# One-block expert visits with tokens as the stationary operand, and small and large visits in turn

## The chip, the cores and the metric

The kernel runs on one core of a Trainium2 chip. The metric is the device time of one launch in microseconds (us); the time before is the median of three runs.

## What is computed

Three stages follow one another: a retention attention (4 batches, 8 heads, 768 positions, head size 64), a dense layer with softplus (3072 tokens, 512 to 2048 to 512), and a mixture of experts with a skip gate. The change is in the last one. Cut to what matters:

```python
def _moe2_ref(x, w_skip, w_gate, w1, w2):
    do_compute = x @ w_skip > 0              # the other tokens pass through
    xc = x[do_compute]
    logits = xc @ w_gate
    e_idx = np.argmax(logits, axis=1)        # one of 8 experts
    gate_w = softmax(logits)[e_idx]
    for e in range(E):
        mask = e_idx == e
        h = np.maximum(xc[mask] @ w1[e], 0.0)        # 512 -> 1024
        y[mask] = gate_w[mask, None] * (h @ w2[e])   # 1024 -> 512
    out[do_compute] = xc + y
```

## The kernel before

The first two stages run in steps over 8 units of 384 tokens and end with every token's expert and place in a list of records. The last stage then makes nine **visits**. A visit is one expert with up to 4 blocks of 128 tokens; `CAPS = (4, 3, 2, 2, 1, 1, 1, 1)` sets the blocks of visits 1 to 8, ranked by the experts' loads, after a first visit of 4 blocks (`first`, visit 0) whose expert is known early. A loop for tokens beyond the caps stands at the end; the trace shows no pass of it.

One visit consists of:

- `load_w1`, `load_w2` (L142): 4 MB of weights, eight pieces of 512 KB, from SP's queue into a ring of ten raw slots. A load waits until the piece ten places before it has been split.
- `gather` (L163): one indirect DMA a block, issued by POOL, fetches token rows.
- `transposes` (L174) and `take` (L936, L937): TensorE turns the tokens of block j into PSUM bank `hp2[j]`; ScalarE copies them out as the high part `xh`, VectorE subtracts to get the low part `xl`.
- `split` (L154, L157): each raw piece becomes a high part `h` (ScalarE) and a low part `l = raw - h` (VectorE for w1, POOL for w2, the eng argument). `h` and `l` have rings of five slots for each layer.
- `ffn1` (L952): each product is the sum of three terms, x-high times w-high, x-high times w-low, x-low times w-high. The weights are the stationary operand (128x128) and the tokens of the visit the moving one, 128 to 512 columns: 96 matmuls whatever the number of blocks. ScalarE (L958) and VectorE (L959) bring the result out as `gh` and `gl`.
- `ffn2` (L968): for each block 24 matmuls with `gh`, `gl` stationary and 512 columns of w2 moving, into bank `op2[j]`.
- `ffn_out` (L976, L979): VectorE scales and adds, POOL scatters the rows to the output.

The order is written out by hand: within a visit, `ffn1` of this visit with the w1 splits of the next, then the next visit's `transposes`, `take` and w2 splits, then `ffn2`. Each engine takes its instructions in that order, so the position in the source sets what waits behind what. The visits run 0, 1, 2, ... 8: the four of one block come last.

```python
for i in range(4):
    ffn1(s, [i])
    if nxt:
        split_w1(nxt, i)
```

Of the kernel before, what the change touches and what calls it, by code (L numbers as in the profile page):

```python
# [38 lines left out]
RAWS, RINGS = 10, {"1": 5, "2": 5}  # L39

# [34 lines left out]
def retention_moe_moe2(ctx: ExitStack, tc: tile.TileContext, a: dict, out: bass.AP):  # L75
# [62 lines left out]

    def load(s, kind, i, src):
        t = s["r" + kind, i] = piece("raw", RAWS, F32)  # L140
        k = KD if kind == "1" else 2
        return nc.sync.dma_start(out=t.rearrange("p (k f) -> p k f", k=k), in_=src)  # L142

    def load_w1(s, e):
        return [load(s, "1", i, wsrc(w1, e)[:, :, i * 256:(i + 1) * 256]) for i in range(4)]
# [4 lines left out]
    def split(s, kind, i, eng, heng=None):  # L150
        r = s["r" + kind, i]
        h, lo = piece("h" + kind, RINGS[kind], F32R), piece("l" + kind, RINGS[kind], F32R)
        if heng is None:
            nc.scalar.activation(out=h, in_=r, func=AF.Copy)  # L154
        else:
            heng.tensor_copy(h, r)
        eng.tensor_tensor(out=lo, in0=r, in1=h.bitcast(F32), op=ALU.subtract)  # L157
        k = KD if kind == "1" else 2
        s["h" + kind, i], s["l" + kind, i] = (x.rearrange("p (k f) -> p k f", k=k) for x in (h, lo))
# [113 lines left out]
    with tc.manual_schedule():  # L273
# [634 lines left out]
        with ExitStack() as left:  # L908
# [9 lines left out]
            xgb.append(xg_p.tile([128, 4, DM], F32, name="xg2"))  # L918
            for n, s in enumerate(vis):
                s["xg"] = xgb[n % 3]  # L920
# [42 lines left out]
            def ffn2(s, blocks=None):  # L963
                for j in range(s["nb"]) if blocks is None else blocks:
                    js = slice(j * 128, (j + 1) * 128)
                    for f in range(NF2):
                        for n, (x, w) in enumerate((("gh", "h2"), ("gl", "h2"), ("gh", "l2"))):
                            nc.tensor.matmul(  # L968
                                op2[j], lhsT=s[x][:, f, js], rhs=s[w, f // 2][:, f % 2, :],
                                start=(f == 0 and n == 0), stop=(f == NF2 - 1 and n == 2),  # L970
                            )

            def ffn_out(s, blocks=None):
                for j in range(s["nb"]) if blocks is None else blocks:
                    op, o = op2[j], s["xg"][:, j, :]
# [65 lines left out]
            ev, _ = known(1)  # L1041
            load_w1(vis[1], ev)
# [14 lines left out]
            load_w2(vis[1], ev)  # L1057
            nc.gpsimd.memset(xgb[2], 0.0)
            gather(vis[1])
            gather(vis[2])  # L1060
            ffn2(first, (0, 1))
            ffn_out(first, (0, 1))
            transposes(vis[1])
            take(vis[1])
            for i in range(4):
                split_w1(vis[1], i)
            ffn2(first, (2, 3))
            ffn_out(first, (2, 3))
            nc.sync.dma_start(out=ovc, in_=a["c_ov"])
            for i in range(4):  # L1070
                split_w2(vis[1], i)
            ev, _ = known(2)
            load_w1(vis[2], ev)
            load_w2(vis[2], ev)
            for n in range(1, NV):
                s = vis[n]
                nxt = vis[n + 1] if n + 1 < NV else None
                if n + 2 < NV:
                    gather(vis[n + 2])
                for i in range(4):  # L1080
                    ffn1(s, [i])
                    if nxt:
                        split_w1(nxt, i)
                if n + 2 < NV:
                    ev, _ = known(n + 2)
                    load_w1(vis[n + 2], ev)
                if nxt:
                    transposes(nxt)
                    take(nxt)
                    for i in range(4):  # L1090
                        split_w2(nxt, i)
                if nxt is None:
                    nov, oti = overflow_table()
                ffn2(s)
                if n + 2 < NV:
                    load_w2(vis[n + 2], ev)
                ffn_out(s)

# [42 lines left out]
```

## Time and profile before

| what | value |
|---|---|
| median of 3 runs | 1042.31 us (1040.92 to 1043.36) |
| the profiled execution's own time | 1038.72 us |
| its span, first to last instruction | 1036.9 us |
| granted TensorE clock, mean over the span | 0.976 |
| busy: TensorE / its weight loads | 94% / 79% |
| busy: VectorE, POOL, ScalarE | 56%, 55%, 46% |
| DMA over the span | 97 GB/s |

The page gives busy shares for the whole span; the change touches only the part after about 805 us, so shares and waits are read from that part. "Chain" is the list of work that ended last, each piece followed back to what released it. In a timeline row, the number in brackets is the idle time of that engine just before, and what ended it.

### The profile page before, as it was taken

The page shows a single profiled execution, that of the slowest core. Times are in us where ns is not written, and L with a number is a line of the kernel's source. Part 1 is how long each engine was busy: PE and PEld are TensorE (multiplying, and loading weights), DVE is VectorE, ACT ScalarE, POOL GpSimd, SP SyncE. Part 2 cuts the span into 40 slices and gives each one's busy share as a digit, 9 for nine tenths or more (in the row PEclk, how much of TensorE's full clock was granted, in tenths as well). Part 3 has the DMA queues.
Part 4 walks back from the last instruction along what each step waited for, and adds up shares of the span by engine and source line. Part 5 has one row for each costly group of instructions (what it writes and reads, how often), then busy time and mean ns, then how long its engine had stood idle before and what let it go on. Part 6 is the DMA issues. An engine that isn't in the chain of part 4 may idle for free.

```text
span 1036.9 us, 16748 instructions
## 1 busy us (share of the span) xinstructions
PE 977.5 (94%) x5922; PEld 822.3 (79%) x5922; DVE 580.8 (56%) x1328; ACT 481.2 (46%) x947; POOL 566.5 (55%) x460
## 2 busy tenths in 40 slices
PE   7877888999999999999999999997989999999994
PEld 6766677888888888888888888886967788999994
DVE  6899995546444654644565465456327452444652
ACT  3554444445354544544544454454544342354650
POOL 5577765546644653654565465455553554366671
PEclk9999899999999999999999999999998999999997
DMA  8744343212310411321041141010054762556830
GB/s 224 189 125 130 101 108 100 46 35 66 88 39 9 117 30 39 100 47 39 12 118 29 27 115 31 9 62 2 1 188 157 256 211 83 173 196 207 258 102 9
DMA packets 186839, 100.50 MB, mean 97 GB/s; under 512 B 140594, under 2 KB 167378, under 8 KB 186752
## 3 DMA queue, kind: packets, MB, share of 16 engines
q1 hardware_dynamic: 182176, 89.56, 31.8%
q0 software_dynamic: 4144, 9.04, 2.6%
q8 instruction: 48, 0.79, 0.3%
q10 hardware_dynamic: 432, 0.79, 0.2%
q14 instruction: 39, 0.32, 0.1%
HBM read 83.43 MB, written 17.85 MB: 98 GB/s over the span
## 4 chain that ended last, share of the span: by engine, by line
PE 67%; DVE 15%; issue 7%; ACT 4%; POOL 4%; DMA 2%; SPq 0%; POOLq 0%; DVEq 0%; ACTq 0%
PE ac L664 20%; PE hp L616 20%; PE hp L952 9%; PE op L968 8%; PE sc L438 3%; PE y L460 3%; DVE lo L652 2%; DVE m L320 2%; DVE m L316 2%; DVE m L324 2%; DVE t L636 1%; DVE g L645 1%; PE y L458 1%; PE tp L689 1%; POOL ln L638 1%
## 5 line engine op out<-in xcount | busy, mean ns | idle before, releaser
L638 POOL TENSOR_TENSOR ln<-ln,t 128x384 f32<-128x384 f32 x127 | 149.7, 1179 | 260.9 <-ACT ln L630 234.0
L664 PE MATMUL ac<-wo,hi 128*128 128x512 f32 x768 | 276.3, 414 | 9.3 <-ACT hi L646 9.3
L616 PE MATMUL hp<-xth,wi 128*128 128x384 f32 x1024 | 212.6, 349 | 0.2 <-ACT xth L484 0.2
L616 PEld LDWEIGHTS hp<-xth,wi 128*128 128x128 f32 x1024 | 176.4, 189 | 12.9 <-ACT xth L484 0.6
L664 PEld LDWEIGHTS ac<-wo,hi 128*128 128x128 f32 x768 | 147.5, 192 | 48.1 <-ACT hi L646 11.1
L628 ACT ACTIVATE u<-hp 128x384 f32<-128x384 f32 x128 | 62.7, 490 | 238.0 <-PE hp L616 219.3
L664 PE MATMUL ac<-wo,lo 128*128 128x512 f32 x384 | 154.7, 403 | 5.0 <-DVE lo L652 4.5
L639 POOL TENSOR_TENSOR ln<-ln,u 128x384 f32<-128x384 f32 x127 | 153.1, 1205 | 10.0
L652 DVE TENSOR_TENSOR lo<-g,hi 128x384 fp32r<-128x384 f32 x128 | 98.2, 767 | 67.4 <-ACT hi L646 65.0
L157 POOL TENSOR_TENSOR l<-raw,h 128x1024 fp32r<-128x1024 f32 x34 | 80.7, 2398 | 65.8 <-ACT h L154 65.7
L616 PE MATMUL hp<-xtl,wi 128*128 128x384 f32 x512 | 109.5, 334 | 0.0
L636 DVE TENSOR_SCALAR t<-u 128x384 f32<-128x384 f32 x128 | 54.0, 422 | 95.6 <-ACT u L629 92.1
L154 ACT ACTIVATE h<-raw 128x1024 fp32r<-128x1024 f32 x71 | 73.2, 1057 | 38.5 <-issue 33.2
L616 PEld LDWEIGHTS hp<-xtl,wi 128*128 128x128 f32 x512 | 90.6, 188 | 0.0
L664 PEld LDWEIGHTS ac<-wo,lo 128*128 128x128 f32 x384 | 74.0, 193 | 20.8 <-DVE lo L652 8.9
L646 ACT ACTIVATE hi<-g 128x384 fp32r<-128x384 f32 x128 | 67.3, 525 | 41.8 <-DVE g L645 35.4
L477 DVE TENSOR_TENSOR wsb<-wps,wsb 64x64 f32<-64x64 f32 x112 | 24.8, 221 | 93.7 <-PE wps L469 93.0
L645 DVE TENSOR_TENSOR g<-g,ln 128x384 f32<-128x384 f32 x128 | 71.6, 559 | 0.9 <-POOL ln L639 0.9
L630 ACT ACTIVATE ln<-u 128x384 f32<-128x384 f32 x128 | 67.4, 527 | 4.1
L629 ACT ACTIVATE u<-u 128x384 f32<-128x384 f32 x128 | 67.2, 525 | 4.1
L958 ACT ACTIVATE gh<-hp 128x128 fp32r<-128x128 f32 (+3 forms) x72 | 28.5, 397 | 77.5 <-PE hp L952 72.9
L157 DVE TENSOR_TENSOR l<-raw,h 128x1024 fp32r<-128x1024 f32 x38 | 55.5, 1470 | 12.3 <-ACT h L154 9.6
(199 smaller groups left out, 1637.1 us busy)
## 6 DMA issues: line engine op xcount, KB each, us to landing
raw<-in_moe_w SPq DMA_DIRECT2D x72, 512.0 KB
raw<-in_moe_w_in SPq DMA_DIRECT2D x16, 512.0 KB
raw<-in_moe_w_out SPq DMA_DIRECT2D x16, 512.0 KB
kn<-in_k SPq DMA_DIRECT2D x56, 96.0 KB
vn<-in_v SPq DMA_DIRECT2D x56, 96.0 KB
x1d<-x SPq DMA_DIRECT2D x21, 256.0 KB
out<-x SPq DMA_DIRECT2D x21, 256.0 KB
ks<-in_k SPq DMA_DIRECT2D x96, 48.0 KB
```

What stands on the lines that cost most here:

```text
L154: nc.scalar.activation(out=h, in_=r, func=AF.Copy)
L157: eng.tensor_tensor(out=lo, in0=r, in1=h.bitcast(F32), op=ALU.subtract)
L616: nc.tensor.matmul(hp, lhsT=wi[:, f, w, kk, :], rhs=x[:, kk, :], start=(n == 0), stop=(n == 3 * KD - 1),)
L630: nc.scalar.activation(out=ln, in_=u, func=AF.Ln, bias=1.0)
L638: eng.tensor_tensor(out=ln, in0=ln, in1=t, op=ALU.subtract)
L639: eng.tensor_tensor(out=ln, in0=ln, in1=u, op=ALU.add)
L645: nc.vector.tensor_tensor(out=g, in0=g, in1=ln, op=ALU.add)
L646: nc.scalar.activation(out=hi, in_=g, func=AF.Copy)
L652: nc.vector.tensor_tensor(out=lo, in0=g, in1=gh[T, f].bitcast(F32), op=ALU.subtract)
L664: nc.tensor.matmul(ac[T, j], lhsT=x[:, js], rhs=wo[:, f, w, :], start=(f == 0 and n == 0), stop=(f == NF - 1 and n == 2),)
L952: nc.tensor.matmul(hp2[(2 * i + g) % 4][:, 0:w], lhsT=wt[:, kk, g * 128:(g + 1) * 128], rhs=x[:, kk, 0:w], start=(n == 0 and kk == 0), sto ...
L968: nc.tensor.matmul(op2[j], lhsT=s[x][:, f, js], rhs=s[w, f // 2][:, f % 2, :], start=(f == 0 and n == 0), stop=(f == NF2 - 1 and n == 2),)
```

## The change

Visits are taken in pairs, a one-block visit and a larger one: (5, 1), (6, 2), (7, 3), (8, 4). In a one-block visit the first layer is `ffn1x`: 128 tokens are the stationary operand and 512 columns of w1 the moving one, so its w1 pieces are loaded by rows of the contraction (4 KB runs) instead of by columns. The result has tokens on partitions, so ScalarE writes `gs` (relu), and `turn` transposes eight 128x128 squares of it into `hp2[0]` and `hp2[1]`, from which `gh` and `gl` are made. The second layer of a one-block visit uses `op2[3]`. Between the two halves of the second layer of the previous large visit stand `turn` and the large visit's own transposes. Two of the four w1 splits of a small visit go to POOL, three of its four w2 splits, and two of the four w2 splits of a large visit (before: no w1 split, all four w2 splits of every visit after the first).

```diff
+PAIRS = ((5, 1), (6, 2), (7, 3), (8, 4))
...
+    def parts_of(s, kind):
+        return 2 if kind == "2" else 1 if s["nb"] == 1 else KD
+
     def load(s, kind, i, src):
         t = s["r" + kind, i] = piece("raw", RAWS, F32)
-        k = KD if kind == "1" else 2
-        return nc.sync.dma_start(out=t.rearrange("p (k f) -> p k f", k=k), in_=src)
+        return nc.sync.dma_start(out=t.rearrange("p (k f) -> p k f", k=parts_of(s, kind)), in_=src)
 
     def load_w1(s, e):
-        return [load(s, "1", i, wsrc(w1, e)[:, :, i * 256:(i + 1) * 256]) for i in range(4)]
+        w = wsrc(w1, e)
+        if s["nb"] == 1:
+            return [load(s, "1", i, w[:, i:i + 1, :]) for i in range(KD)]
+        return [load(s, "1", i, w[:, :, i * 256:(i + 1) * 256]) for i in range(4)]
...
-            xgb.append(xg_p.tile([128, 4, DM], F32, name="xg2"))
-            for n, s in enumerate(vis):
-                s["xg"] = xgb[n % 3]
+            xgs = [xg_p.tile([128, 1, DM], F32, name=f"xs{i}") for i in range(2)]
+            for n, (a1, b1) in enumerate(PAIRS):
+                vis[a1]["xg"], vis[b1]["xg"] = xgs[n % 2], xgb[(n + 1) % 2]
+            gs = g_p.tile([128, F2], F32, name="gs")
...
-            def ffn2(s, blocks=None):
+            def ffn1x(s, kk):
+                for g in range(2):
+                    for n, (x, w) in enumerate((("xh", "h1"), ("xh", "l1"), ("xl", "h1"))):
+                        nc.tensor.matmul(
+                            hp2[2 + g], lhsT=s[x][:, kk, 0:128], rhs=s[w, kk][:, 0, g * 512:(g + 1) * 512],
+                            start=(kk == 0 and n == 0), stop=(kk == KD - 1 and n == 2),
+                        )
+
+            def ffn1x_out():
+                for g in range(2):
+                    nc.scalar.activation(out=gs[:, g * 512:(g + 1) * 512], in_=hp2[2 + g], func=AF.Relu)
+
+            def turn(s):
+                s["gh"] = g_p.tile([128, NF2, 128], F32R, name="gh1")
+                s["gl"] = g_p.tile([128, NF2, 128], F32R, name="gl1")
+                for b in range(2):
+                    for f in range(4):
+                        nc.tensor.transpose(hp2[b][:, f * 128:(f + 1) * 128], gs[:, (4 * b + f) * 128:(4 * b + f + 1) * 128], ident)
+                for b in range(2):
+                    fs, tv = slice(4 * b, 4 * b + 4), hp2[b].rearrange("p (f t) -> p f t", f=4)
+                    nc.scalar.activation(out=s["gh"][:, fs, :], in_=tv, func=AF.Copy)
+                    nc.vector.tensor_tensor(out=s["gl"][:, fs, :], in0=tv, in1=s["gh"][:, fs, :].bitcast(F32), op=ALU.subtract)
+
+            def ffn2(s, blocks=None, ops=None):
                 for j in range(s["nb"]) if blocks is None else blocks:
                     js = slice(j * 128, (j + 1) * 128)
-                    for f in range(NF2):
+                    op = op2[3 if s["nb"] == 1 else j]
+                    for f in range(NF2) if ops is None else ops:
                         for n, (x, w) in enumerate((("gh", "h2"), ("gl", "h2"), ("gh", "l2"))):
                             nc.tensor.matmul(
-                                op2[j], lhsT=s[x][:, f, js], rhs=s[w, f // 2][:, f % 2, :],
+                                op, lhsT=s[x][:, f, js], rhs=s[w, f // 2][:, f % 2, :],
                                 start=(f == 0 and n == 0), stop=(f == NF2 - 1 and n == 2),
                             )
 
             def ffn_out(s, blocks=None):
                 for j in range(s["nb"]) if blocks is None else blocks:
-                    op, o = op2[j], s["xg"][:, j, :]
+                    op, o = op2[3 if s["nb"] == 1 else j], s["xg"][:, j, :]
...
+            def fetch(n, which):
+                if n not in ids:
+                    ids[n] = known(n)[0]
+                (load_w1 if which == 1 else load_w2)(vis[n], ids[n])
+
+            fetch(PAIRS[0][0], 1)
...
-            load_w2(vis[1], ev)
-            nc.gpsimd.memset(xgb[2], 0.0)
-            gather(vis[1])
-            gather(vis[2])
+            fetch(PAIRS[0][1], 1)
+            for x in xgs:
+                nc.gpsimd.memset(x, 0.0)
+            gather(vis[PAIRS[0][0]])
+            gather(vis[PAIRS[0][1]])
             ffn2(first, (0, 1))
             ffn_out(first, (0, 1))
-            transposes(vis[1])
-            take(vis[1])
+            s1, b1 = (vis[n] for n in PAIRS[0])
+            transposes(s1)
+            take(s1)
             for i in range(4):
-                split_w1(vis[1], i)
-            ffn2(first, (2, 3))
-            ffn_out(first, (2, 3))
-            nc.sync.dma_start(out=ovc, in_=a["c_ov"])
-            for i in range(4):
-                split_w2(vis[1], i)
-            ev, _ = known(2)
-            load_w1(vis[2], ev)
-            load_w2(vis[2], ev)
-            for n in range(1, NV):
-                s = vis[n]
-                nxt = vis[n + 1] if n + 1 < NV else None
-                if n + 2 < NV:
-                    gather(vis[n + 2])
+                split_w1(s1, i, nc.gpsimd if i % 2 else nc.vector)
+            ffn2(first, (2,))
+            ffn_out(first, (2,))
+            big = first
+            for m, (ns, nb) in enumerate(PAIRS):
+                s, b = vis[ns], vis[nb]
+                nxt = PAIRS[m + 1] if m + 1 < len(PAIRS) else None
+                fetch(ns, 2)
+                for kk in range(KD):
+                    ffn1x(s, kk)
+                    split_w1(b, kk)
+                ffn1x_out()
+                if m == 0:
+                    last = (3,)
+                    ffn2(big, last, range(4))
+                else:
+                    last = (big["nb"] - 1,)
+                    ffn2(big, range(big["nb"] - 1))
+                    ffn_out(big, range(big["nb"] - 1))
+                if nxt:
+                    gather(vis[nxt[0]])
+                turn(s)
+                split_w2(s, 0)
+                transposes(b)
+                take(b)
+                ffn2(big, last, range(4, NF2) if m == 0 else None)
+                for i in range(1, 4):
+                    split_w2(s, i, nc.gpsimd if i % 2 else nc.vector)
+                ffn_out(big, last)
+                if m == 0:
+                    nc.sync.dma_start(out=ovc, in_=a["c_ov"])
+                if nxt:
+                    fetch(nxt[0], 1)
+                fetch(nb, 2)
+                if nxt:
+                    fetch(nxt[1], 1)
                 for i in range(4):
-                    ffn1(s, [i])
+                    ffn1(b, [i])
                     if nxt:
-                        split_w1(nxt, i)
-                if n + 2 < NV:
-                    ev, _ = known(n + 2)
-                    load_w1(vis[n + 2], ev)
+                        split_w1(vis[nxt[0]], i, nc.gpsimd if i % 2 else nc.vector)
                 if nxt:
-                    transposes(nxt)
-                    take(nxt)
-                    for i in range(4):
-                        split_w2(nxt, i)
-                if nxt is None:
-                    nov, oti = overflow_table()
-                ffn2(s)
-                if n + 2 < NV:
-                    load_w2(vis[n + 2], ev)
+                    gather(vis[nxt[1]])
+                    transposes(vis[nxt[0]])
+                    take(vis[nxt[0]])
+                for f in range(0, NF2, 2):
+                    ffn2(s, ops=(f, f + 1))
+                    split_w2(b, f // 2, nc.gpsimd if f % 4 else nc.vector)
                 ffn_out(s)
+                big = b
+            nov, oti = overflow_table()
+            ffn2(big)
+            ffn_out(big)
```

How the order moves, at three places. First TensorE, in the first layer of a one-block visit (the last pieces of a visit; `hp` is a bank of results, `xh`, `xl` the tokens, `h`, `l` the w1 parts, the stationary operand stands last). Before, one output chunk after another:

```order
L952 MATMUL hp_0_8232<-xh_10472,h_0_10414 128x128 x4
L952 MATMUL hp_0_8232<-xh_10472,l_0_10415 128x128 x4
L952 MATMUL hp_0_8232<-xl_10473,h_0_10414 128x128 x4
L952 MATMUL hp_1_8233<-xh_10472,h_0_10414 128x128 x4
L952 MATMUL hp_1_8233<-xh_10472,l_0_10415 128x128 x4
L952 MATMUL hp_1_8233<-xl_10473,h_0_10414 128x128 x4
```

and now:

```order
L972 MATMUL hp_2_8234<-h_1_10125,xh_10139 128x512
L972 MATMUL hp_2_8234<-l_1_10126,xh_10139 128x512
L972 MATMUL hp_2_8234<-h_1_10125,xl_10140 128x512
L972 MATMUL hp_3_8235<-h_1_10125,xh_10139 128x512
L972 MATMUL hp_3_8235<-l_1_10126,xh_10139 128x512
L972 MATMUL hp_3_8235<-h_1_10125,xl_10140 128x512
```

A quarter of the layer was 24 matmuls of 128 columns and is 6 of 512. Second, TensorE in the fourth pair, between the two blocks of the previous visit's second layer (`gs` is the result to be turned, `xg` the gathered tokens of the large visit):

```order
L998 MATMUL op_0_8446<-h_2_10179,gl_10000 128x512
L998 MATMUL op_0_8446<-l_2_10180,gh_9999 128x512
L986 MATMUL hp_0_8232<-cst,gs 128x128 x4
L986 MATMUL hp_1_8233<-cst,gs 128x128 x4
L179 MATMUL hp_0_8232<-cst,xg_8259 128x128 x4
L179 MATMUL hp_1_8233<-cst,xg_8259 128x128 x4
L998 MATMUL op_1_8447<-h_4_10149,gh_9999 128x512
L998 MATMUL op_1_8447<-h_4_10149,gl_10000 128x512
```

The same two banks are filled twice in a row: the second filling has to wait until the first has been read. Third, VectorE from the end of pair three to that place:

```order
L163 TENSOR_TENSOR l_4_10150<-raw_9973,h_4_10149 128x1024
L163 TENSOR_TENSOR l_1_10170<-raw_9977,h_1_10169 128x1024
L1006 SCALAR_TENSOR_TENSOR xs_8377<-op_3_8570,rc_8787,xs_8377 128x512
L163 TENSOR_TENSOR l_2_10202<-raw_9991,h_2_10201 128x1024
L163 TENSOR_TENSOR l_3_10212<-raw_9993,h_3_10211 128x1024
L163 TENSOR_TENSOR l_4_10222<-raw_9995,h_4_10221 128x1024
L163 TENSOR_TENSOR l_0_10232<-raw_9997,h_0_10231 128x1024
L1006 SCALAR_TENSOR_TENSOR xg_8260<-op_0_8446,rc_8699,xg_8260 128x512
L990 TENSOR_TENSOR gl_10266<-hp_0_8232,gh_10265 128x512
L990 TENSOR_TENSOR gl_10266<-hp_1_8233,gh_10265 128x512
```

The two `gl` rows that free the banks now stand behind six splits on VectorE, while POOL has the splits between them.

## Rows read from the trace of the kernel before

**Rows 1.** The page, busy time of the whole span.
```profile
PE 977.5 (94%) x5922; PEld 822.3 (79%) x5922; DVE 580.8 (56%) x1328; ACT 481.2 (46%) x947; POOL 566.5 (55%) x460
```

**Rows 2.** Chain from 820 us: start, length (us), engine, tile, line, count.
```profile
909.99 11.51 PE hp L952 x96
...
956.18 10.67 PE hp L952 x96
966.85 0.46 PE hp L174 x4
967.31 5.48 PE op L968 x24
...
989.40 2.64 PE hp L952 x24
...
997.63 0.04 issue
...
1000.57 0.46 PE hp L174 x4
```

**Rows 3.** Timeline of `ffn2`, weight load and matmul: start, length (us), engine, line.
```profile
985.15 0.19 PEld L968 LDWEIGHTS op<-h,gl 128*128 128x128 f32 x1
985.15 0.39 PE L968 MATMUL op<-h,gh 128*128 128x512 f32 x1
```

**Rows 4.** Groups by form, 820 us to the end: busy us, mean ns of one.
```profile
L154 ACT ACTIVATE h<-raw 128x1024 fp32r<-128x1024 f32 x64 | 66.2, 1058 | 38.5 <-issue 33.2 <-PE op L968 4.3 <-ACT h L154 1.0
...
L976 DVE SCALAR_TENSOR_TENSOR xg<-op,rc,xg 128x512 f32<-128x512 f32 x15 | 11.3, 751 | 52.2 <-PE op L968 47.4 <-POOL l L157 4.8
...
L937 DVE TENSOR_TENSOR xl<-hp,xh 128x512 fp32r<-128x512 f32 x15 | 9.7, 683 | 0.0
...
L936 ACT ACTIVATE xh<-hp 128x512 fp32r<-128x512 f32 x14 | 7.7, 596 | 0.0
```

**Rows 5.** Timeline at the hand-over from visit 0 to visit 1.
```profile
816.72 1.47 PE L174 MATMUL hp<-cst,xg 128*128 128x128 f32 x12
...
819.20 2.07 ACT L936 ACTIVATE xh<-hp 128x512 fp32r<-128x512 f32 x4 [12.57 <-PE hp L174]
819.59 0.66 PE L174 MATMUL hp<-cst,xg 128*128 128x128 f32 x4 [1.41 <-DMA xg<-x1d,rc]
```

**Rows 6.** Line 157 on VectorE and on POOL: ns shortest/median/longest.
```profile
L157 DVE TENSOR_TENSOR l<-raw,h x38: 1209/1225/5555, 779.5 to 1001.9; 128x1024 fp32r<-128x1024 f32 x38
L157 POOL TENSOR_TENSOR l<-raw,h x34: 2367/2396/2479, 797.7 to 1010.4; 128x1024 fp32r<-128x1024 f32 x34
```

**Rows 7.** Timeline of visit 7: four POOL splits, and VectorE beside them.
```profile
986.91 9.42 POOL L157 TENSOR_TENSOR l<-raw,h 128x1024 fp32r<-128x1024 f32 x4
...
991.03 0.29 DVE L959 SCALAR_TENSOR_TENSOR gl<-hp,gh 128x128 fp32r<-128x128 f32 x1 [0.84 <-ACT gh L958]
...
993.32 4.10 DVE L157 TENSOR_TENSOR l<-raw,h 128x1024 fp32r<-128x1024 f32 x1 [0.66 <-ACT h L154]
...
997.67 0.52 PEld L952 LDWEIGHTS hp<-xh,h 128*128 128x128 f32 x4 [0.43 <-DVE gl L959]
```

**Rows 8.** Stretches: length, busy PE, PEld, DVE, ACT, POOL, clock, DMA share, GB/s.
```profile
945.00:956.00 11.00, 11.00 (x51) 9.11 (x50) 3.00 (x4) 5.81 (x7) 5.29 (x3) 1.00 0.52 159
...
973.00:984.00 11.00, 11.00 (x100) 10.96 (x100) 8.13 (x12) 5.29 (x12) 7.85 (x4) 1.00 0.82 239
984.00:990.00 6.00, 6.00 (x32) 5.08 (x30) 2.49 (x4) 4.99 (x6) 4.64 (x3) 1.00 0.88 295
```

**Rows 9.** Waits of SP's queue, 760 us to the end: us, times, longest.
```profile
SPq L142 <- POOL l L157: 80.6, 26, 15.4
```

**Rows 10.** Timeline, the last matmul and the last scatter.
```profile
1022.33 0.39 PE L968 MATMUL op<-l,gh 128*128 128x512 f32 x1
...
1023.79 0.99 POOL L979 DMA_INDIRECT out<-xg,rc  x1 [9.87 <-DVE xg L976]
```

**Rows 11.** Timeline of POOL, a gather that waits for an earlier scatter.
```profile
966.73 1.05 POOL L163 DMA_INDIRECT xg<-x1d,rc  x1 [3.22 <-DMA out<-xg,rc]
```

More of the change, by code (lines that the diff above doesn't have):

```diff
@@ L157, in split @@
         eng.tensor_tensor(out=lo, in0=r, in1=h.bitcast(F32), op=ALU.subtract)
-        k = KD if kind == "1" else 2
-        s["h" + kind, i], s["l" + kind, i] = (x.rearrange("p (k f) -> p k f", k=k) for x in (h, lo))
+        s["h" + kind, i], s["l" + kind, i] = (x.rearrange("p (k f) -> p k f", k=parts_of(s, kind)) for x in (h, lo))
     def gather(s, rows=NT):
@@ L1040, in retention_moe_moe2 @@
             split_w1(first, 3)
-            ev, _ = known(1)
-            load_w1(vis[1], ev)
+            ids = {}
+            def fetch(n, which):
[3 more added lines that the diff above has]
+            fetch(PAIRS[0][0], 1)
             ffn1(first, [1])
```

## The prediction

> **What bounds the kernel now.** I began with the page: TensorE is busy 94% of the span, no other engine over 56% beside its weight loads [rows 1]. That is an average over three stages, so I read the chain of the stage that changes. From 820 us it is TensorE, piece after piece without gaps: first layer, transposes, second layer, next visit [rows 2]. The reader should compare two of its lengths. The second layer of one block takes 5.48 us for 24 matmuls, 0.228 us each; the first layer of the same block takes 10.67 us for 96 matmuls, 0.111 us each. The multiplications are as many. Each matmul has its own weight load of 0.19 us, laid over the matmul before it [rows 3]: with 512 columns moving it is hidden, with 128 it leaves the array half idle. So TensorE sets the end here, and its first layer in the four one-block visits is twice as long as the arithmetic asks. The one long gap is the hand-over from visit 0 to visit 1: 1.41 us until a gather lands [rows 5]. DMA runs at 239 to 295 GB/s where SP has free slots [rows 8], and TensorE does not wait for it; SP waits for slots, 80.6 us of it on POOL's splits [rows 9].
>
> **The change, part by part.**
>
> *First layer of four one-block visits.* Before: three times 10.67 us, and once 11.17 us (989.40 to 1000.57, visit 7, with a stall) [rows 2], together 43.2 us. Now 24 matmuls each, with a weight load of 128x128 and 512 columns of fp32r, the form of the second layer; at its 5.48 us that is 21.9 us. Gain 21.3 us, all on the chain. (The Trainium skill, page "TensorE: Matmul & The Clock Gate", section "Back-to-back issue gap", gives a sustained spacing of about 81 ns at 128 columns and 131 ns at 512. By it the gain would be an estimated 4 x (96 x 81 - 24 x 131) ns = 18.5 us. The rows say 111 and 228 ns for this data type, and I go by them.)
>
> *Turning the result.* Eight transposes a visit; four take 0.46 us [rows 2], so 0.92 us, four times: 3.7 us lost.
>
> *The two banks filled twice.* `turn` fills `hp2[0]` and `hp2[1]`, and the large visit's transposes fill the same two at once after it. Before, `hp2[0]` had half a first layer's time to be emptied. Now the chain is: four transposes and their tail, about 0.63 us; ScalarE copies 0.60 us; VectorE subtracts 0.68 us [rows 4]; three hand-overs of 0.04 us [rows 2]: 2.03 us, while TensorE is ready after 0.92. Wait 1.1. The second bank is free 0.68 us later, at 2.72, and TensorE comes at 2.47: another 0.3. Together 1.4 us a pair, 5.6 us over four. Bounds: 0.9 us if the second wait hides, 2.5 us if one ScalarE split of 1.06 us [rows 4] gets ahead; I take 1.4, since nothing is queued on ScalarE between the relu and this copy. After it the second layer of the large visit's last block (5.48 us, 2.7 in pair 1) covers `take`.
>
> *Hand-over from visit 0.* Only one gather, not four, must land before the first transposes; it is issued first, and three gathers had landed by 816.72 us [rows 5]. The 1.41 us go.
>
> *The first small visit.* It starts 0.46 + 5.48 us after 816.72, at 822.7 us, one block's second layer earlier than visit 1's did. Its w1 pieces must be split by then. If ScalarE's copies start at 819.20 as in the row [rows 5], the four high parts end at 820.9 to 824.0, and the low parts, two on VectorE and two on POOL, which do not run together (see rivals), end with the third piece at up to 828.1; TensorE wants it at 825.6: 2.5 us. If the copies start when the transposes end, it is 0.7 us. I take 2.5, the end that a row shows.
>
> *Splits and slots.* Per pair 16 pieces on ScalarE at 1.06 us, nine on VectorE at 1.22, seven on POOL at 2.40 [rows 4, 6]: 17, 11 and 17 us under pairs of 36 us and more, so covered on the average. TensorE's pair 4, the shortest, is 5.48 (first layer) + 5.48 + 3.2 (turn, transposes, wait) + 5.48 + 11.51 (large first layer [rows 2]) + 5.48 = 36.6 us; pair 3, with one block more and the next visit's transposes, 42.5. I cost these moves at nothing. The cover is thinnest at pair 4's `turn`. Counted from the start of pair 3's small second layer: POOL ends its last w1 split at about 3.6 us, two gathers (1.3 us each with their issue [rows 11]) at 6.2 and two w2 splits at 11.0; if VectorE's four w1 splits wait for all of that, they end at 15.9. `turn` comes at 3 x 5.48 = 16.4, and VectorE's first subtraction there 1.3 us later.
>
> *Loads.* The order of loads is the order of splits, ten pieces ahead, as before; 8.4 MB a pair over 36.6 us is 229 GB/s, below the rates of [rows 8]. Nothing on the chain. The memsets before the first gathers shrink from one of 2048 to two of 512 columns, off the chain.
>
> *The end.* The last matmul, VectorE, the scatter 1.5 us after it [rows 10], and the rest of the span stay: the last block is now one of two, but its scatter is alone at the end.
>
> *Sum.* -21.3 + 3.7 + 5.6 - 1.4 + 2.5 = -10.9 us. The profiled execution goes from 1038.72 to 1027.8. It lies 3.6 us below the median of the runs shown, so for the median I say 1042.3 - 10.9 = **1031.4 us**.
>
> **The rivals.**
>
> *A. Splits that lock each other out.* VectorE's splits are usually 1.22 us, but one took 5.55 [rows 6]; one took 4.10 us, from 993.32 to 997.42, and came free when POOL's row of four ended at 996.33, after which TensorE waited 0.43 us [rows 7]. A subtraction from PSUM (0.29 us at 991.03) ran at full speed beside POOL. So a VectorE split waits for a whole run of POOL splits, and the change puts splits on both at once and the bank-freeing subtraction behind them. For it: a gather can hold POOL back 3.2 us first [rows 11]. Against it: in pairs 2 and 3 the margin is over 5 us. Price: POOL's run late by 3.2 us costs 3.2 - 1.8 = 1.4 us at pair 4's `turn`, and one POOL split of 2.4 us out of turn costs as much in the last second layer, which starts right behind the splits of its own weights; with one more stall of 0.4 us as in [rows 7], 4.2 us. Time 1035.6. (The Trainium skill, page "SBUF — State Buffer", section "Who interferes with whom", says that a VectorE instruction with two SBUF inputs and a GpSimd instruction that reads SBUF lock each other out for the whole instruction, whoever issues first. By that rule the trace agrees for VectorE. It also says that POOL waits in the other order; no row shows it, for POOL's 34 splits all take 2367 to 2479 ns.)
>
> *B. Slower: the transfers become the bound in pairs 3 and 4.* If loads came only at the 159 GB/s of the stretch 945 to 956 [rows 8], each pair would need 52.7 us, 10 and 16 us over TensorE's. Time 1042.3 - 10.9 + 26 = 1057. It decides below 187 GB/s (2 x 8.39 MB in 42.5 + 36.6 + 10.9 us). For it: slots are freed by later, mixed splits. Against: that stretch was short of slots, not of transfers, and 239 to 295 GB/s were reached just behind it.
>
> *C. The change does not do what it says:* a new weight for every matmul not hidden, 24 x (0.228 + 0.19) = 10 us, so that turning is lost outright: 1050. The second layer already changes its weight each time and shows 0.228 [rows 2, 3].
>
> *D. More gain:* start covered (0.7 us) and the second bank wait hidden (2 us): about 1028.
>
> *E. No change:* A and part of B together eat 11 us: 1042.
>
> **How the numbers follow.** My forecast 0.62, A 0.20, D 0.07, B 0.05, E 0.04, C 0.02. About 0.2% (2 us) is what a measurement tells from no change; the three runs spread by 0.23%. Faster is the forecast, A and D: 0.89; same E: 0.04; slower B and C: 0.07. Range: downward 21.3 + 1.4 - 3.7 - 3.6 - 0.7 = 14.7 us of gain with both bounds, 1027.6, and a run's spread of 1.4 below: 1026.2. Upward A with a run's spread of 1.4: 1037.0.
>
> **What would show it.** First layers of small visits at 5.5 us, in 24 matmuls 0.228 us apart. Gaps of about 1.1 and 0.3 us before the large visit's transposes, ended by VectorE's `gl`, four times. No gather wait near 817 us and a wait of 0.7 to 2.5 us on splits near 824. TensorE's last matmul near 1011.5 us, the clock at 1.00. I am wrong if a gap over 3 us ended by a split or by a transfer stands in pairs 2 to 4 (A, B), if the small first layers take over 6 us (C), or if the stage before 805 us moves.

## The result and the profile after

| | before | after |
|---|---|---|
| median, runs taken together | 1042.68 us (4 runs, 1040.92 to 1043.36) | 1025.63 us (4 runs, 1024.97 to 1026.17) |
| profiled execution / its span | 1038.72 / 1036.9 us | 1025.38 / 1023.6 us |
| granted clock, mean | 0.976 | 0.975 |

The ratio is 0.984 with an interval of 0.9822 to 0.9859: faster, by 1.6% and by more than forecast. 1031.4 us was said, with a range from 1026.2; the time lies 5.8 us below the forecast and 0.6 below the range.

The page's busy times, which answer to [rows 1]: TensorE's busy time fell by 12.7 us, with 256 matmuls fewer (four times 96 became 24 and 8).

```profile
PE 964.8 (94%) x5666; PEld 804.6 (79%) x5666; DVE 600.8 (59%) x1308; ACT 482.5 (47%) x931; POOL 565.0 (55%) x457
```

The chain after, from the hand-over to the second small visit, and below it the turning of pair 3 (start, length, engine, tile, line, count), answers to [rows 2]:

```profile
818.57 0.44 PE hp L179 x4
819.01 5.49 PE op L998 x24
824.50 5.44 PE hp L972 x24
829.94 2.72 PE op L998 x12
832.66 0.45 PE hp L986 x4
...
833.13 0.61 ACT gh L989
...
833.76 0.70 DVE gl L990
...
834.51 2.12 PE hp L179 x16
836.64 2.77 PE op L998 x12
839.40 21.76 PE hp L958 x96
...
867.09 5.44 PE hp L972 x24
...
936.77 0.45 PE hp L986 x4
...
938.62 1.25 PE hp L179 x8
```

The small visit's first layer (L972) takes 5.44 us instead of 10.67, all four times. Between the halves of the large visit's second layer the chain leaves TensorE: it goes over ScalarE's `gh` and VectorE's `gl` before the transposes (L179) can start. TensorE's waits from 800 us on, in one row for its matmuls and one for its weight loads (total, times, longest), show nothing else:

```profile
PE hp L179 <- DVE gl L990: 3.9, 4, 1.0
...
PEld hp L179 <- DVE gl L990: 5.6, 8, 1.2
```

The timeline at the hand-over and in pair 4 (start, length, engine, line; idle time before in brackets), beside [rows 5] and [rows 6, 7]:

```profile
818.41 0.60 PE L179 MATMUL hp<-cst,xs 128*128 128x128 f32 x4
819.05 0.60 ACT L942 ACTIVATE xh<-hp 128x512 fp32r<-128x512 f32 x1 [10.71 <-PE hp L179]
819.54 4.84 ACT L160 ACTIVATE h<-raw 128x1024 fp32r<-128x1024 f32 x5
...
821.62 5.85 POOL L163 TENSOR_TENSOR l<-raw,h 128x1024 fp32r<-128x1024 f32 x2 [0.97 <-ACT h L160]
822.52 2.69 DVE L163 TENSOR_TENSOR l<-raw,h 128x1024 fp32r<-128x1024 f32 x1 [0.67 <-ACT h L160]
...
963.60 9.80 DVE L163 TENSOR_TENSOR l<-raw,h 128x1024 fp32r<-128x1024 f32 x4
...
964.14 4.76 POOL L163 TENSOR_TENSOR l<-raw,h 128x1024 fp32r<-128x1024 f32 x2
...
973.73 0.75 DVE L1006 SCALAR_TENSOR_TENSOR xg<-op,rc,xg 128x512 f32<-128x512 f32 x1 [0.33 <-PE op L998]
974.79 1.29 DVE L990 TENSOR_TENSOR gl<-hp,gh 128x512 fp32r<-128x512 f32 x2 [0.31 <-ACT gh L989]
...
980.51 2.15 DVE L163 TENSOR_TENSOR l<-raw,h 128x1024 fp32r<-128x1024 f32 x1 [2.36 <-ACT h L160]
...
981.92 3.01 POOL L163 TENSOR_TENSOR l<-raw,h 128x1024 fp32r<-128x1024 f32 x1 [0.33 <-ACT h L160]
...
1011.20 0.98 POOL L1009 DMA_INDIRECT out<-xg,rc  x1 [3.01 <-DVE xg L1006]
```

At 818 us TensorE waits for no gather, and ScalarE starts right behind the transposes. VectorE's second split there, the third piece of w1, is held by POOL's (2.69 us instead of 1.22) and ends at 825.2; TensorE asks for that piece half-way through its first layer, at 827.2, and waits for nothing. In pair 4 the four splits that should take 4.9 us take 9.80, the length of POOL's two on top; VectorE is idle for 0.33 and 0.31 us before the subtraction that frees the bank. The lock of rival A is there, and came within 0.6 us of costing something. The two rows of 980 and 982 us are used further down.

From the start of the hand-over's transposes to the last scatter of the output the kernel before takes 1023.79 - 816.72 = 207.1 us [rows 5, 10] and the changed one 1011.20 - 818.41 = 192.8: 14.3 us less. The two profiled executions differ by only 13.3 us: the hand-over came 1.7 us later in the second (818.41 against 816.72), and the stretch from the start of the last scatter on, in which the traces show no other work, was 0.7 us shorter (12.4 against 13.1).

### The profile page after: what moved, and what is told of

Its sections match the earlier page's. It is cut to its first block, busy times and chain, and to the rows that moved or that the text cites. A ratio compares the mean times of both kernels' runs of the same rounds, so it can differ in the third digit from the quotient of the medians.

```text
span 1023.6 us, 16220 instructions
## 1 busy us (share of the span) xinstructions
PE 964.8 (94%) x5666; PEld 804.6 (79%) x5666; DVE 600.8 (59%) x1308; ACT 482.5 (47%) x931; POOL 565.0 (55%) x457
## 4 chain that ended last, share of the span: by engine, by line
PE 71%; DVE 15%; issue 5%; ACT 4%; POOL 2%; DMA 1%; SPq 0%; DVEq 0%; POOLq 0%; ACTq 0%
PE ac L669 20%; PE hp L621 20%; PE op L998 9%; PE hp L958 8%; PE sc L443 3%; DVE lo L657 3%; PE y L465 3%; DVE m L325 2%; PE hp L972 2%; DVE m L321 2%; DVE m L329 2%; PE y L463 1%; DVE g L650 1%; DVE t L641 1%; PE tp L694 1%
## 5 line engine op out<-in xcount | busy, mean ns | idle before, releaser
L163 POOL TENSOR_TENSOR l<-raw,h 128x1024 fp32r<-128x1024 f32 x30 | 77.2, 2582 | 54.7 <-ACT h L160 32.5
L163 DVE TENSOR_TENSOR l<-raw,h 128x1024 fp32r<-128x1024 f32 x42 | 77.0, 1860 | 14.4 <-ACT h L160 14.1
L636 ACT ACTIVATE g<-hp 128x384 f32<-128x384 f32 x128 | 60.6, 473 | 0.0
```

## The experiments

Each is timed in turn with the kernel before; "before" in this table is its median in the same job. The intervals are those of the ratio. Rows with the same "before" were timed together; a difference between rows with another one also carries the difference of those medians, up to 1.6 us.

| run | time, us (lowest to highest) | before | ratio |
|---|---|---|---|
| before once more | 1039.54 (1038.21 to 1045.96) | 1040.56 | 1.0006 (0.9986 to 1.0026) |
| form alone | 1035.80 (1034.83 to 1036.93) | 1040.56 | 0.9948 (0.9929 to 0.9968) |
| order alone | 1043.28 (1041.87 to 1045.76) | 1040.56 | 1.0023 (1.0008 to 1.0037) |
| banks apart | **1019.78** (1019.24 to 1020.54) | 1040.56 | 0.9798 (0.9773 to 0.9822) |
| small gather last | 1027.40 (1026.45 to 1029.62) | 1041.76 | 0.9872 (0.9849 to 0.9895) |
| hand-over late | 1038.34 (1036.34 to 1043.94) | 1041.76 | 0.9976 (0.9957 to 0.9994) |
| before, no POOL splits | 1037.81 (1035.53 to 1038.63) | 1041.76 | 0.9964 (0.9950 to 0.9978) |
| order alone, no POOL splits | 1037.37 (1035.57 to 1038.80) | 1041.76 | 0.9966 (0.9950 to 0.9981) |
| banks woven | 1020.25 (1018.91 to 1021.11) | 1040.17 | 0.9803 (0.9781 to 0.9825) |
| banks apart, no POOL splits | 1020.81 (1019.99 to 1021.50) | 1040.17 | 0.9808 (0.9786 to 0.9830) |
| before, six profiled executions | 1038.13 to 1040.71 | | |

**Before once more.** No edit.

> The kernel before, unchanged, profiled again. The changed kernel gained 17.0 us by the medians, but only 13.3 us between the two profiled spans (1036.9 and 1023.6 us). Theory (the first profile of before caught a short execution, and the shortness lies in the stages ahead of the hand-over): this profile shows a span of about 1040 us, the hand-over from visit 0 near 819 to 820 us instead of 816.7, and the same 205.6 us from there to the last matmul. Rival (the last stage of before is usually longer than in the first profile, by waits that it does not show): hand-over near 817 us, and 208 to 210 us from there to the last matmul.

Its 12 executions lie between 1038.21 and 1045.96 us and the 25 of the kernel before beside them between 1037.83 and 1044.64, while the changed kernel's four lie within 1.2 us. So the three runs that the forecast started from lay high, and their median was no fixed distance from the profiled execution. Neither expectation came true: this profile is as short as the first (span 1036.7 us), and the last stage is not longer. Its timeline at the hand-over, beside [rows 5]:

```profile
817.41 1.47 PE L174 MATMUL hp<-cst,xg 128*128 128x128 f32 x12
...
818.05 1.57 ACT L936 ACTIVATE xh<-hp 128x512 fp32r<-128x512 f32 x3 [10.72 <-PE hp L174]
...
819.57 0.66 PE L174 MATMUL hp<-cst,xg 128*128 128x128 f32 x4 [0.69 <-DMA xg<-x1d,rc]
```

The wait for the gather is 0.69 us here, not 1.41, and ScalarE starts 0.64 us after the first transposes, not 2.48. In all eight profiles of the kernel before (six more stand further down) the gather wait lies between 0.46 and 1.41 us; the row that the forecast used is the longest. ScalarE's start is 0.63 to 0.64 us after the first transposes in three of the eight and 2.45 to 2.54 us in five, and it does not follow the length of that wait. Two of them, with nearly equal waits (0.57 us in the last of those six, 0.58 us in their second):

```profile
817.14 1.47 PE L174 MATMUL hp<-cst,xg 128*128 128x128 f32 x12
819.59 2.07 ACT L936 ACTIVATE xh<-hp 128x512 fp32r<-128x512 f32 x4 [12.54 <-PE hp L174]
```

```profile
817.89 1.47 PE L174 MATMUL hp<-cst,xg 128*128 128x128 f32 x12
818.52 1.57 ACT L936 ACTIVATE xh<-hp 128x512 fp32r<-128x512 f32 x3 [10.72 <-PE hp L174]
```

In the traces whose hand-over transposes run without a wait between them, the changed kernel's among them, ScalarE always starts 0.63 to 0.67 us after the first. What held it for the other 1.8 us in the five is not shown.

**Form alone.** The old order of visits and the old distribution of splits, with the new first layer for visits 5 to 8:

```diff
+            for n in range(5, NV):
+                s, p = vis[n], vis[n - 1]
...
+                for kk in range(KD):
+                    ffn1x(s, kk)
...
+                ffn1x_out()
...
+                turn(s)
```

> Form without the alternation: visits in the old order 1 to 8, the four one-block visits with tokens stationary and turned, each one's second layer moved behind the next one's first layer so that no bank is filled twice in a row; splits as before (w1 on VectorE, w2 on POOL). Theory (TensorE's matmul time is the gain, and alternation only gives the other engines time): a small visit is then 5.44 + 0.44 + 5.49 + 0.9 = 12.3 us of TensorE, but POOL's four splits (9.6 us) and VectorE's four (4.9 us) cannot overlap, and with POOL's gathers and scatters they need some 15 to 16 us, so small visits take 15 to 16 us instead of 16.6 and the kernel lands at 1035 to 1040 us. Rival (alternation gives nothing): four visits of 12.3 us, no bank waits, hand-over as before: 1023 to 1026 us.

1035.80 us. Two middle small visits in a row took 12.3 and 13.3 us in the trace, not the 15 or 16 expected: splits and loads keep up better than that. What is lost is lost elsewhere, a good part of it by my arrangement of the gather buffers (two large ones instead of three): TensorE's waits and the clock there (the windows' columns: length, PE, PEld, DVE, ACT, POOL, clock, DMA share, GB/s):

```profile
925.01 1.09 PE L179 MATMUL hp<-cst,xg 128*128 128x128 f32 x4 [2.88 <-DMA xg<-x1d,rc]
927.08 1.09 PE L179 MATMUL hp<-cst,xg 128*128 128x128 f32 x4 [0.98 <-DMA xg<-x1d,rc]
```

```profile
924.00:928.00 4.00, 2.01 (x9) 1.67 (x10) 1.51 (x2) 0.60 (x1) 1.57 (x2) 0.62 0.88 304
928.00:932.00 4.00, 4.00 (x11) 3.12 (x11) 0.69 (x1) 1.55 (x2) 2.17 (x1) 0.53 0.12 49
```

So this run does not say what the new form is worth in a well arranged old order.

**Order alone.** The pairs with their mixed splits, and the old first layer in the small visits:

```diff
                 for kk in range(KD):
-                    ffn1x(s, kk)
+                    ffn1(s, [kk])
                     split_w1(b, kk)
-                ffn1x_out()
...
-                turn(s)
```

> Alternation without the new form: pairs (5,1), (6,2), (7,3), (8,4) and the splits on both engines as changed, but one-block visits keep the old first layer of 96 matmuls with 128 columns, loads by columns, and nothing is turned. Theory (the order by itself only removes the gather wait of 1.4 us and the stall of 0.5 us in visit 7): 1039 to 1041 us. Rival (alternation carries a large part of the 17 us, by loads and splits spread evenly): 1030 to 1036 us.

1043.28 us, slower than the kernel before and outside what the theory and the rival said. The profile is of the longest execution, 1045.76 us. Pair 2's small first layer in the timeline, and the windows around it:

```profile
874.82 4.71 POOL L161 TENSOR_TENSOR l<-raw,h 128x1024 fp32r<-128x1024 f32 x2
...
875.85 4.78 DVE L161 TENSOR_TENSOR l<-raw,h 128x1024 fp32r<-128x1024 f32 x1 [0.65 <-ACT h L158]
...
880.55 0.47 DVE L963 SCALAR_TENSOR_TENSOR gl<-hp,gh 128x128 fp32r<-128x128 f32 x2
...
880.88 0.66 PE L956 MATMUL hp<-xh,h 128*128 128x128 f32 x4 [0.96 <-DVE gl L963]
```

```profile
880.00:882.00 2.00, 1.12 (x10) 1.12 (x11) 2.00 (x4) 1.18 (x2) 1.52 (x1) 1.00 0.82 285
882.00:884.00 2.00, 2.00 (x13) 2.00 (x12) 1.89 (x5) 0.28 (x1) 0.00 (x0) 0.59 0.98 292
884.00:886.00 2.00, 2.00 (x8) 1.81 (x8) 0.29 (x1) 1.00 (x2) 0.00 (x0) 0.50 0.89 308
886.00:888.00 2.00, 2.00 (x6) 1.52 (x6) 1.22 (x1) 1.17 (x2) 0.00 (x0) 0.50 1.06 382
888.00:890.00 2.00, 2.00 (x8) 1.57 (x7) 0.00 (x0) 0.00 (x0) 0.00 (x0) 0.71 0.97 291
```

One VectorE split of 1.22 us lasts 4.78, because POOL's two run; the subtraction that frees the bank stands behind it; TensorE is idle 0.96 us. Then the granted clock goes to 0.50, the level of 1.2 GHz, for some 7 us in all, and the second layer behind it takes 18.48 us where it takes 16.43 in the run without POOL splits below. The old form needs VectorE in the middle of a first layer, to free its banks; the new one does not. In this trace the lock of rival A acts on the form that the change removes.

**Order alone, no POOL splits,** and **before, no POOL splits.** One line more in both:

```diff
+        eng = eng if s is first else nc.vector
         eng.tensor_tensor(out=lo, in0=r, in1=h.bitcast(F32), op=ALU.subtract)
```

> The pairs with the old first layer (measured 1043.28 us), now with all splits of visits 1 to 8 on VectorE. Theory (its loss is the lock: a VectorE split of 4.8 us beside POOL's two, the bank-freeing subtraction behind it, TensorE idle for 1 us, and then a clock of 0.50 for 6 us): waits on that subtraction go, the clock stays at 1.00, and the time falls to 1036 to 1039 us, just under the kernel before. Rival (alternation itself costs, by the order of the queues): 1042 to 1045 us as before.

> The kernel before with all splits of visits 1 to 8 on VectorE and none on POOL, so that no split can lock another out. Theory (the lock costs the old order almost nothing, since its TensorE chain has only a 0.4 us wait on it): within 1 us of the kernel before, 1039.5 to 1041.5 us, or longer by what a queue of eight splits on VectorE costs. Rival (the lock makes the spread of the kernel before): the spread falls under 3 us and the median to 1036 to 1038.

1037.37 and 1037.81 us: the pairs gain 5.9 us by it, and the waits on the subtraction are gone. From the hand-over's transposes to the last scatter their trace is 5.2 us shorter (205.1 us against 210.2). For the kernel before it was the rival that came true, and my theory that fell: it gains 4 us, and of 12 executions none is over 1038.63, while 15 of the 29 beside them are over 1041.7. Its trace shows little of that gain: the same stretch, from the hand-over's last transposes on, takes 203.7 us instead of 204.2, and the stretch from the last scatter on is over 1 us shorter. The edit also gives each of these splits to the engine that needs 1.22 us for one instead of 2.40, and leaves POOL free for gathers and scatters; for the kernel before, no run separates these from the lock. Without POOL's splits the two orders cost the same within the noise (0.4 us between the medians), so no run shows a gain from taking visits in pairs by itself.

**Hand-over late.** The kernel before, with visit 1's transposes one block's second layer later:

```diff
+            ffn2(first, (2,))
+            ffn_out(first, (2,))
             transposes(vis[1])
             take(vis[1])
...
-            ffn2(first, (2, 3))
-            ffn_out(first, (2, 3))
+            ffn2(first, (3,))
+            ffn_out(first, (3,))
```

> The kernel before with one thing changed: the transposes of visit 1 stand one block's second layer (5.5 us) later, so that its gathers have landed. Theory (the gather wait at the hand-over, and a clock that falls after it in some executions, make the kernel before spread over 7 us): the wait is gone, the spread falls under 3 us, and the median falls from 1040.6 to 1036 to 1038 us. Rival (the spread comes from the stages before 800 us or from the splits in the visits): the shortest executions gain about 1 us, the spread stays at 6 us or more and the median at 1039 to 1041.

1038.34 us, between what the theory and the rival said. The gather wait is gone from the trace and the shortest executions are about 2 us shorter, but 2 of 12 still reach 1042.5 and 1043.9. The gather is part of the difference and not the whole source of the spread. Long executions are fewer here (2 of 12 over 1041.7, against 15 of the 29 beside them); whether the moved transposes did that, 12 executions do not settle.

**Small gather last.** The reverse, in the changed kernel:

```diff
-            gather(vis[PAIRS[0][0]])
             gather(vis[PAIRS[0][1]])
+            gather(vis[PAIRS[0][0]])
```

> The changed kernel with one thing undone: the four gathers of the large visit are issued before the one gather of the first small visit, so that the hand-over waits for the fifth gather instead of the first. Theory (the hand-over's gather wait is where the kernel before loses time that the forecast counted as only 1.4 us, and it is this wait that differs from execution to execution): TensorE waits 1 to 4 us at the hand-over, the executions spread by 3 us or more (changed kernel: 1.2 us), median 1027 to 1030 us. Rival (the hand-over is worth no more than the 1.4 us of one profile, or nothing): median 1025.6 to 1027.1, spread under 2 us.

1027.40 us, 1.8 more than the changed kernel, at the lower end of what the theory said; the spread goes from 1.2 to 3.2 us. TensorE's waits show the price:

```profile
PE hp L179 <- DMA xs<-x1d,rc: 2.2, 1, 2.2
```

**Before, six profiled executions,** to see a long one. No edit.

> The kernel before, one profile more. Its 54 executions so far lie between 1037.8 and 1044.9 us, and neither of the two profiles shows a long one. Theory (a long execution is one in which a VectorE split is held by POOL's): if this one is over 1041 us, it shows TensorE waits of over 1 us on the subtraction behind such a split, and a clock under 1.00 after one. Rival: it shows a wait of over 2 us for the gather at the hand-over, or the time lies before 800 us. If it is under 1040 us, the last stage is that of the first profile.

> The kernel before, a second profile more, for the same question: over 1041 us, theory says waits of over 1 us behind a held VectorE split and a clock under 1.00 after them, the rival a gather wait of over 2 us or lost time before 800 us. Under 1040 us it says nothing new.

> The kernel before, one profile more: some two in five of its executions are over 1041 us, and no profile so far shows one. If this one is over 1041 us, theory says that the time is lost in visits 5 to 8 behind a VectorE split that POOL holds, with TensorE waiting over 1 us for the subtraction behind it and the clock under 1.00 after that; the rival says a gather wait of over 2 us at the hand-over, or time lost before 800 us. Under 1040 us it says nothing new.

The other three asked the same. None is long: 1038.13 to 1040.71 us. In all eight profiles of the kernel before, the stretch from the hand-over's last transposes to the last scatter is within 0.1 us of 204.2 (1023.79 - 819.59 in the first), with the same 0.3 us wait on `gl`. In the longest of them, 1040.71 us, the chain has the same stretch later:

```profile
821.76 0.65 PE hp L174 x4
...
1025.91 0.98 POOL out L979
```

So what these eight differ by, up to 2.6 us, lies ahead of these transposes, the gather wait among it. What an execution of 1042 to 1046 us of this kernel looks like was not seen.

**Banks apart.** The changed kernel, with the large visit's tokens turned into banks 2, 3, 0, 1:

```diff
-                nc.tensor.transpose(hp2[j][:, ks], s["xg"][:, j, ks], ident)
+                nc.tensor.transpose(hp2[(j + off) % 4][:, ks], s["xg"][:, j, ks], ident)
...
-                transposes(b)
-                take(b)
+                transposes(b, 2)
+                take(b, 2)
```

> The changed kernel with one edit: the large visit's transposes after the turning fill the banks 2, 3, 0, 1 instead of 0, 1, 2, 3. Theory (TensorE waits at each turning for ScalarE's copy and VectorE's subtraction, about 1.3 us a pair, and this wait is on the path): 4 to 5 us less, 1020.5 to 1021.5 us, and the four waits of 1.0 us ended by gl fall under 0.3 us. Rival (the wait is repaid later, since what follows waits for the splits anyway): 1025 to 1026 us, with new waits of about 1 us on splits or on take.

1019.78 us, 5.85 us less than the changed kernel, a little more than the theory said, and a kernel faster than both. Of this the trace shows 4.6 us as bank waits: from the hand-over's transposes to the last scatter it takes 188.0 us (817.63 to 1005.63), the changed kernel 192.6 (818.57 to 1011.20). Another 0.9 us of the two profiles' difference lies ahead of the hand-over, where nothing was edited, so the bank waits are worth 4.6 us and not 5.85. In the chain of pair 3 the eight turning transposes, the eight of the next visit and the second layer follow one another:

```profile
817.63 0.44 PE hp L179 x4
...
933.94 0.87 PE hp L986 x8
934.81 0.87 PE hp L179 x8
935.69 5.49 PE op L998 x24
...
1005.63 0.98 POOL out L1009
```

**Banks woven.** The same, and in pairs 1 and 2 part of the second layer between the transposes of blocks 0, 1 and the rest:

```diff
-                transposes(b, 2)
+                rest = range(4, NF2) if m == 0 else range(NF2)
+                cut = (rest[0] + NF2) // 2 if b["nb"] > 2 else rest[0]
+                transposes(b, 2, range(min(2, b["nb"])))
+                if cut > rest[0]:
+                    ffn2(big, last, range(rest[0], cut))
+                    transposes(b, 2, range(2, b["nb"]))
                 take(b, 2)
-                ffn2(big, last, range(4, NF2) if m == 0 else None)
+                ffn2(big, last, range(cut, NF2))
```

> The version with the large visit's transposes in the other two banks (measured 1019.78 us), and in the pairs where the large visit has 3 or 4 blocks half of what is left of the previous visit's second layer moved between the transposes of blocks 0, 1 and those of blocks 2, 3. Theory (the two waits left there, 1.4 us each, are bank waits that any 1.4 us of second layer covers): 1017.0 us (1016.2 to 1017.8). Rival (what stands after the last transposes, 1.4 us in pair 1, no longer covers taking the tokens out, 0.60 and 0.68 us a block): 1018.4 or no gain at all, 1019.8.

1020.25 us, no gain in the median. I had misread the chain of banks apart: in pairs 1 and 2 it passes over ScalarE and VectorE for 1.4 us, but TensorE is doing transposes meanwhile. TensorE's waits in banks apart were small all along, and only in weight loads:

```profile
PEld hp L179 <- DVE gl L990: 0.9, 3, 0.3
```

In banks woven they are gone, and its last stage is 0.7 us shorter (187.3 us against 188.0); so small a gain is lost in the spread of the executions.

**Banks apart, no POOL splits.** The line on `eng` above, in that version.

> The version with the large visit's transposes in the other two banks (measured 1019.78 us), with all splits of visits 1 to 8 on VectorE. Theory (the new first layer needs no subtraction of VectorE within it, so a split that is locked out holds nothing that TensorE waits for): 1018.8 to 1020.8 us, no change. Rival (the lock still costs here as it does the old form, where taking POOL's splits away gave 3 to 6 us): 1014 to 1017 us. Slower, 1021 or more, if VectorE's longer queue reaches a turning.

1020.81 us: nothing gained. What gave 6 us with the old first layer gives none with the new one.

## Why the forecast was too high

The steps, in the order of the prediction:

- **First layers: right.** 43.2 us became 4 x 5.44 = 21.8 (21.9 said), 0.227 us a matmul. Rival C is out. The 131 ns at 512 columns that the Trainium skill gives ("TensorE: Matmul & The Clock Gate", section "Back-to-back issue gap") are not reached here either.
- **Turning: right.** 0.87 us a visit in the version where nothing waits there, 3.5 in all (3.7 said).
- **Two banks filled twice: right.** Turning and the transposes of pair 3 take 0.45 + 0.02 + 0.61 + 0.02 + 0.70 + 0.04 + 1.25 = 3.1 us, from 936.77 to 939.88, instead of 1.74 without waits: 1.4 us a pair, as said. In the traces banks apart gave 4.6 us of it back (5.6 said) and kept 0.8 in pairs 1 and 2.
- **Hand-over: right in kind.** The gather wait is gone; with the gather last, a wait of 2.2 us is there. Its price of 1.41 us was the longest of eight profiles.
- **"I take 2.5, the end that a row shows": wrong, and the first of two errors.** The first small visit waits 0. I took ScalarE's start from one row, 819.20, 2.48 us after the first transposes, in a hand-over whose wait the paragraph before had just taken away. Such a late start stands in five of the eight profiles of the kernel before and in no trace without that wait. After the change it starts 0.64 us after them (818.41, 819.05), as in the second profile of the kernel before; and even the other bound, 0.7 us, was too much. (A slip beside it: from 822.7 half a first layer leads to 825.4 us, not 825.6, so the row would have given a wait of 2.7 us.)
- **"It lies 3.6 us below the median of the runs shown, so for the median I say 1042.3 - 10.9": wrong, the second error.** It assumes that what lies between the profiled execution and the median stays. For the changed kernel it is 0.25 us (1025.63 - 1025.38). The kernel before has executions 3 to 7 us longer than its shortest, the changed one has none among the four timed, and its three versions with the banks apart none among 15. Part of this error is luck of the draw: the kernel before had medians of 1039.54 to 1041.76 us later on, which would have put the forecast 0.6 to 2.8 us lower. The two errors, 2.5 and 3.3 us, are the whole miss of 5.8; against the profiled executions alone, 1038.72 to 1025.38, the other terms of the sum, -13.4 us, are what was measured, -13.3, partly by luck: the last stage gained 14.3, the stages ahead of it ran 1.7 us later in that execution, and the end from the last scatter on was 0.7 us shorter.
- **Splits, loads, clock: right.** TensorE waited for neither splits nor transfers (B out), and the clock was 1.00 in the last stage.
- **Rival A: seen, and free.** POOL now waits too: its split at 981.92 took 3.01 us beside a VectorE split that began at 980.51, where [rows 6] had none above 2.48. By the rule that the prediction named (the Trainium skill, "SBUF — State Buffer", section "Who interferes with whom": the one that comes second waits), the trace agrees in this order as well. The lock makes splits late; it makes TensorE late only beyond a slack, and in pair 4, where the forecast looked for it, 0.6 us of that was left.

Why the old kernel's executions differ is shown in part. Taking POOL's splits away took the long ones away, and the same edit took a seen stall with a lowered clock out of the pairs. In the eight profiles the gather wait differs by 0.95 us and all that lies ahead of the hand-over's last transposes by up to 2.6. That a long execution of the kernel before is a held split followed by a low clock fits these runs and the lower mean clock of the longest ones (0.971 to 0.974 in all 18 over 1043 us whose clock is on record, mostly 0.977 and more below 1040); by an estimate from the window rows above, some 7 us at 0.50 lower the mean by 0.003, about the difference. It does not fit the executions just below: eight of the 13 between 1042 and 1043 us have 0.978 or 0.979. No profile of a long one was had, and it stays open.

## What to carry to other kernels

A term that removes a wait changes the start of all that stood behind it: work the next term from the new start, not from the old row. Look at how far single executions of the kernel before spread; a median above the profile is partly the draw of a few executions and partly a cost that the change may remove, so it is no constant to be carried over. When two engines exclude each other, what counts is not how often but what TensorE has queued behind the one that waits: a form that needs no help inside a layer can afford the lock.

## What the runs showed of the hardware

An idle time of TensorE of 0.96 us in the middle of a first layer was followed by a clock of 0.50 for some 7 us, while four of 1.0 us before the transposes of the changed kernel were not, though TensorE ran without gaps on both sides in both kernels. The window of the first of those four and the one behind it (length, PE, PEld, DVE, ACT, POOL, clock, DMA share, GB/s):

```profile
832.00:836.00 4.00, 3.02 (x23) 2.44 (x23) 1.46 (x3) 2.83 (x5) 0.75 (x1) 1.00 1.02 403
836.00:840.00 4.00, 4.00 (x22) 3.37 (x21) 3.02 (x5) 4.00 (x6) 3.25 (x2) 1.00 0.83 264
```

So the price of such a wait was the wait alone in one kernel and several times as much in the other: the two layers around the wait of 0.96 us took 4.4 us more (13.03 and 18.48 us) than in the run without POOL splits (10.67 and 16.43). The trace of one execution tells only which it was there. And a POOL split that started beside a VectorE split took 0.6 us longer, until that one had ended: the lock works both ways.
